# Holding side jobs to their place in the queue, splitting new weights behind the old ones' last products, and regrouping the differences of w2

## The chip, the cores and the metric

The kernel runs on one core of a Trainium2 chip. The metric is device time in microseconds (us) of one execution; three executions were timed, and one more was profiled.

## What is computed

The reference is a block-sparse attention (4 batches, 8 heads, 768 positions, head size 64), whose output, 3072 rows of 512, goes through a mixture of eight experts in which every row takes every expert:

```python
logits = x @ w_gate
P = np.exp(logits - logits.max())
for _ in range(8):
    P /= P.sum(1, keepdims=True) + 1e-09
    P /= P.sum(0, keepdims=True) + 1e-09
    P *= N / E
for e in range(E):
    h = np.maximum(x @ w1[e], 0.0)
    out += P[:, e:e + 1] * (h @ w2[e])
```

with x of 3072 x 512, w1[e] of 512 x 1024 and w2[e] of 1024 x 512, all float32.

## The kernel before

Attention runs first, to about 465 us; the rest is the mixture of experts (MoE), which the change concerns.

**Numbers.** Each float32 operand is held as a high and a low half in float16 (`h`, `w1p`, `w2p`, and x in `xp`), and a product takes three matmuls: high by high, high by low, low by high. A weight is first scaled by a power of two: eight maxima on VectorE (`mx_w`, line 187), one over them (193), a transpose on TensorE that spreads it (`all_w`, 110) and some short steps (199 to 205). Its high half comes from ScalarE (line 1011), its low half from VectorE (1015), 1024 columns each: such a pair is a split.

**Products.** Both stages use seven products in place of eight for a 2 x 2 blocked matrix product, in the order p = 0, 1, 5, 6, 3, 4, 2, so that sums and differences are needed on both sides: of weights on POOL (`queue_sum`, line 1026), of h on POOL and VectorE, and of results on VectorE.

**Stages and batches.** There are 32 batches i = (e, b), eight experts times four groups of rows. `stage1(i, qi)` makes one quarter of h: seven products of six matmuls (128 x 384, line 1135, tiles p), each read from its bank by a comb (VectorE, line 1145) or ScalarE. From the combs come the terms of h: relu on ScalarE, s and three more on POOL (lines 1207, 1033), high halves on ScalarE (1155), low halves on POOL or VectorE (1159, 1165). `stage2(i, p)` is one of seven products in three slices of twelve matmuls (128 x 256, line 1248, tiles py), and VectorE adds each slice into the result (acc, line 1269, 512 or 256 columns). The loop mixes the seven products of `stage2(i)` with the four quarters of `stage1(i + 1)`. There are four banks for p and four for py.

**Weights.** A raw weight lies in one buffer (`r`, one copy), first w1 of the next expert and, when that is split, w2 (load: line 173). The split halves overwrite the old expert's: `w1p` may be written once the last quarter of the expert's last batch has used it, `w2p` once its last stage two has. So in the last batch of an expert (b = 3) the kernel must split w1, load, measure and split w2, and go on with products.

**What sets the order.** The class `Slots` has two queues: `urgent` (sums and low halves of h) and `lazy` (weights: maxima, splits and sums). `tick`, called after each product or slice, adds what a product costs on TensorE, VectorE and ScalarE to running totals, and calls the jobs whose delay is over and whose charge (`dve=`, `act=`, `pool=`) fits under the total of TensorE plus a lead. `need` calls what a product must have. What they call is then in program order, but the framework's scheduler places each engine's instructions anew by when it simulates them to be ready, so a job may come to stand ahead of instructions that were called before it. `keep_in_program_order` holds the side jobs among themselves only.

Of the kernel before, what the change touches and what calls it, by code (L numbers as in the profile page):

```python
# [55 lines left out]
def tile_sparse_attention_moe(  # L56
# [951 lines left out]
    def queue_split(dst, src, key, delay=1):  # L1008
# [31 lines left out]
    def split_w1(e):  # L1040
# [5 lines left out]
        one(0, a[0, 0])  # L1046
        queue_sum(a[0, 0], a[1, 0], a[0, 0], ("w1", e, 5))
        one(1, a[0, 1])
        queue_sum(a[0, 1], a[0, 1], a[0, 0], ("w1", e, 2))
        one(5, a[0, 0])  # L1050
        one(6, s3)
        one(3, a[1, 1])
        one(4, a[1, 0])
        one(2, a[0, 1])

    def split_w2(e, r):
# [10 lines left out]
        one(0, m[0, 0])  # L1067
        queue_sum(m[0, 0], m[0, 1], m[0, 0], ("w2", e, 4))
        one(1, m[1, 0])
        queue_sum(t2, m[1, 1], m[0, 0], ("w2", e, 5))  # L1070
        queue_sum(m[0, 1], m[0, 1], m[1, 1], ("w2", e, 6))
        queue_sum(m[1, 0], m[1, 0], t2, ("w2", e, 3))
# [317 lines left out]
```

## Time and profile before

| | |
|---|---|
| median of 3 runs | 2357.71 us (2354.69 to 2358.62) |
| profiled execution | 2357.4 us, of which its span 2355.6 us |
| mean granted TensorE clock | 0.986 of full speed |
| TensorE / VectorE / ScalarE / POOL busy | 2200.1 / 2014.4 / 1256.0 / 1287.1 us |

The profile is of one execution. Its span is counted from the first to the last instruction, 1.8 us shorter than the execution's own time. Line numbers are those of the kernel before; engines are PE (TensorE matmul), PEld (its weight load), DVE (VectorE), ACT (ScalarE), POOL (GpSimd) and SP (the queue that issues loads). A wait is put down to the instruction whose end released it. Neighbouring instructions of one engine overlap by some 0.08 us, so that the step from start to start is a little shorter than a duration.

### The profile page before, as it was taken

Reading aid. Unit: us, or ns where it says so; the run is one execution under the profiler, and the core shown is the slowest. Engines: PE = TensorE matmul, PEld = TensorE weight load, DVE = VectorE, ACT = ScalarE, POOL = GpSimd, SP = SyncE. Lnnn points to the kernel's source line nnn. Section 1 sums busy time; section 2 is a strip of 40 time slices with the busy share of each in tenths; the row PEclk is TensorE's granted clock in tenths of the full one; section 3 lists DMA queues with packets and bytes.
Section 4 is the critical chain, followed back from the end, with each engine's and each line's share of the span. In section 5 each row is a group of like instructions: output and inputs, shape, how many; then the busy total and the mean of one; then the engine's idle time right before and its main releaser. Section 6 shows DMA issues by size and latency. Waiting matters only on the chain.

```text
span 2355.6 us, 47334 instructions
## 1 busy us (share of the span) xinstructions
PE 2200.1 (93%) x18892; PEld 1608.6 (68%) x18892; DVE 2014.4 (86%) x3570; ACT 1256.0 (53%) x2173; POOL 1287.1 (55%) x1235
## 2 busy tenths in 40 slices
PE   5999998879999999999989999999899999998999
PEld 3766666647666677677667776776677667766777
DVE  8999999888789878987898789878987898789876
ACT  4888878655465445444444445444544454445442
POOL 2012334496367645765576557655865486548543
PEclk9999999999999999999999999999999999999999
DMA  6667765422121212121212121212211221121221
GB/s 152 135 123 151 186 131 121 135 97 75 48 82 50 83 48 83 48 83 48 83 48 83 48 84 52 80 48 83 64 68 48 84 80 52 48 84 48 75 75 54
DMA packets 191888, 192.34 MB, mean 82 GB/s; under 512 B 131740, under 2 KB 144052, under 8 KB 191668
## 3 DMA queue, kind: packets, MB, share of 16 engines
q1 hardware_dynamic: 191104, 189.30, 28.2%
q8 instruction: 147, 2.41, 0.4%
q14 instruction: 73, 0.60, 0.1%
q10 hardware_dynamic: 564, 0.03, 0.0%
HBM read 140.54 MB, written 17.30 MB: 67 GB/s over the span
## 4 chain that ended last, share of the span: by engine, by line
PE 57%; DVE 21%; POOL 9%; issue 6%; DMA 4%; ACT 3%; SPq 0%; DVEq 0%; POOLq 0%; ACTq 0%
PE py L1248 25%; PE p L1135 23%; POOL r L1026 3%; DVE top L673 3%; DMA r<-in_moe_w_dram 3%; DVE h L1165 2%; PE u L731 2%; POOL h L1165 2%; DVE u L1145 2%; DVE acc L1269 2%; DVE mx_w L187 2%; PE t L697 1%; PE m L664 1%; PE t L700 1%; PE m L667 1%
## 5 line engine op out<-in xcount | busy, mean ns | idle before, releaser
L1248 PE MATMUL py<-w2p,h 128*128 128x256 f16 x8064 | 971.1, 275 | 52.7 <-ACT h L1155 23.7
L1248 PEld LDWEIGHTS <-h 128*128 128x128 f16 x8064 | 790.1, 99 | 209.9 <-ACT h L1155 28.8
L1269 DVE SCALAR_TENSOR_TENSOR acc<-py,spare,acc 128x256 f32<-128x256 f32 (+1 forms) x840 | 459.2, 581 | 49.5 <-PE py L1248 46.9
L1165 POOL TENSOR_TENSOR h<-u,h 128x384 f16<-128x384 f32 x128 | 127.0, 992 | 601.3 <-ACT h L1155 601.3
L1135 PEld LDWEIGHTS <-attic 128*128 128x128 f16 x3072 | 301.8, 98 | 195.9 <-issue 22.5
L1135 PE MATMUL p<-attic 128*128 128x384 f16 x2304 | 413.2, 328 | 16.4 <-DVE r L1145 14.4
L1135 PE MATMUL p<-arena 128*128 128x384 f16 x2304 | 407.6, 327 | 19.4 <-DVE a L1145 11.2
L1135 PEld LDWEIGHTS <-arena 128*128 128x128 f16 x2304 | 225.9, 98 | 153.5 <-issue 24.8
L1155 ACT ACTIVATE h<-c 128x384 f16<-128x384 f32 x256 | 133.6, 522 | 330.7 <-DVE c L1145 256.7
L705 ACT ACTIVATE pe<-t,shift,qk 128x768 int32<-128x768 f32 x192 | 189.7, 989 | 78.6 <-PE t L700 73.0
L1145 DVE SCALAR_TENSOR_TENSOR a<-p,a 128x384 f32<-128x384 f32 x384 | 211.1, 550 | 18.9 <-PE p L1135 14.3
L673 DVE TENSOR_REDUCE top<-m 128x1 f32<-128x768 f32 x192 | 181.8, 949 | 16.7 <-PE m L667 16.4
L1155 ACT ACTIVATE h<-r 128x384 f16<-128x384 f32 x256 | 132.5, 521 | 66.5 <-POOL r L1033 63.0
L1207 POOL TENSOR_TENSOR s<-a,u 128x384 f32<-128x384 f32 x128 | 129.6, 1013 | 68.7 <-ACT a L1204 68.7
L1033 POOL TENSOR_TENSOR r<-s,r 128x384 f32<-128x384 f32 x128 | 155.4, 1214 | 9.6
L1033 POOL TENSOR_TENSOR c<-c,r 128x384 f32<-128x384 f32 x128 | 150.8, 1178 | 10.0
L1135 PE MATMUL p<-arena,attic 128*128 128x384 f16 x768 | 146.1, 327 | 0.0
L1026 POOL TENSOR_TENSOR r<-r 128x256 f32<-128x256 f32 (+1 forms) x106 | 135.0, 1290 | 20.0 <-DVE arena L1015 17.9
L664 PE MATMUL m<-kt,qt 128*128 128x512 f16 (+1 forms) x384 | 129.6, 338 | 14.5 <-DVE top L673 7.2
L1165 POOL TENSOR_TENSOR h<-r,h 128x384 f16<-128x384 f32 x128 | 142.8, 1115 | 0.2 <-ACT h L1155 0.2
L1145 DVE SCALAR_TENSOR_TENSOR r<-p,a 128x384 f32<-128x384 f32 x128 | 70.7, 552 | 79.0 <-PE p L1135 59.4
L697 PE MATMUL t<-qt,kt 128*128 128x512 f16 (+1 forms) x384 | 127.9, 333 | 10.8 <-DVE top L673 10.6
(206 smaller groups left out, 3683.1 us busy)
## 6 DMA issues: line engine op xcount, KB each, us to landing
arena<-xd SPq DMA_DIRECT2D x128, 384.0 KB, 3.9
attic<-xd SPq DMA_DIRECT2D x96, 384.0 KB, 3.9
r<-in_moe_w_dram SPq DMA_DIRECT2D x16, 2048.0 KB, 8.4
arena<-in_q_dram SPq DMA_DIRECT2D x16, 384.0 KB, 4.5
arena<-in_k_dram SPq DMA_DIRECT2D x16, 384.0 KB, 4.8
arena<-in_v_dram SPq DMA_DIRECT2D x4, 1536.0 KB, 8.5
xd<-xs_t SPq DMA_DIRECT2D x16, 384.0 KB, 4.6
out_dram<-acc SPq DMA_DIRECT2D x24, 256.0 KB, 2.0
```

The costliest lines, as they stand in the source:

```text
L664: nc.tensor.matmul(sc[:, lo:hi], lhsT=qt[:, 0, c], rhs=ka[:, lo:hi], start=True, stop=False)
L673: nc.vector.tensor_reduce(out=tops[n][:, c : c + 1], in_=sc[:, :S], axis=AX.X, op=ALU.max)
L697: nc.tensor.matmul(sc[:, lo:hi], lhsT=kt[:, 0, c], rhs=qa[:, lo:hi], start=True, stop=False)
L705: nc.scalar.activation(pe, sc[:, :S], AF.Exp, bias=shift, scale=qk[n // 2][3])
L1026: lambda c=c: Pinned.gpsimd.tensor_tensor(out=out[:, c], in0=x[:, c], in1=y[:, c], op=op),
L1033: nc.gpsimd.tensor_tensor(out=out, in0=x, in1=y, op=ALU.subtract)
L1135: nc.tensor.matmul(ps, lhsT=w1p[p][:, l, kc, fs], rhs=xp[p][:, r, kc], start=(kc == 0 and m == 0), stop=(kc == KH - 1 and m == 2),)
L1145: nc.vector.scalar_tensor_tensor(out=t, in0=ps, scalar=HDOWN, in1=other, op0=ALU.mult, op1=ALU.add)
L1155: nc.scalar.activation(h[:, 0], src, AF.Relu if relu else AF.Copy)
L1165: eng.tensor_tensor(out=h[:, 1], in0=src, in1=h[:, 0], op=ALU.subtract)
L1248: nc.tensor.matmul(py, lhsT=hs[i, p, kc][:, l, tsl], rhs=w2p[p][:, r, kc], start=(kc == 0 and m == 0), stop=(kc == KF // 2 - 1 and m == 2),)
L1269: nc.vector.scalar_tensor_tensor(out=dst, in0=src, scalar=c, in1=dst, op0=ALU.mult, op1=ALU.add)
```

## The change

1. `not_earlier(fn)`: when a lazy job of a weight (keys `scale`, `w1`, `w2`) is called, each instruction it makes on VectorE, ScalarE or POOL is tied to the last instruction of its engine that was called before it and is no side job. The tie is one of order on the same engine and brings no wait on a semaphore; the scheduler can place the job later, but not ahead of that instruction.
2. `split_w1` returns its jobs by product and in pairs with their differences; `stage1` calls those of p behind the product p, in the last quarter of the last batch that uses the old weight (`used`). Before, all jobs were queued at the start of the expert's last batch's loop round. The order of the new weight's parts is 0, 1, 6, 5, 3, 4, 2, and no longer 0, 1, 5, 6, 3, 4, 2.
3. Load, maxima and first jobs of w2 are queued ahead of the next batch's first quarter, not behind it.
4. `split_w2` forms its differences in another way: t1 = m01 − m00 and m01 − m11 need no scale and are queued with the maxima; the two others, m11 − t1 and m10 less that, follow the first split. Product 4's source is now t1, product 5's is in m00. There are still four differences.
5. Charges and delays: a maximum 0.65 for 0.6 (first delay 8 for 6), a high half 1.1 for 1.04, a low half 1.4 for 1.2, a difference 3.2 for 2.4, a low half of h on POOL 1.05 for 0.9, the sums of h 4.4 for 3.9.

```diff
+    def not_earlier(fn):
+        made = nc.cur_bb.bb.instructions
+        n = len(made)
+        fn()
+        for ins in list(made[n:]):
+            if ins.engine not in SIDE:
+                continue
+            for old in reversed(made[:n]):
+                if old.engine == ins.engine and old.name not in aside:
+                    tc.add_manual_dep(ins, old.name, behind, reason="not_ahead_of_its_place")
+                    break
+            aside.add(ins.name)
...
-            fn, _, _, costs, _ = queue.pop(n)
+            fn, key, _, costs, _ = queue.pop(n)
+            self.charge(costs)
...
-            self.charge(costs)
-            fn()
+            if key[0] in ("scale", "w1", "w2"):
+                not_earlier(fn)
+            else:
+                fn()
...
-        t2 = raw.tile([P, h, DH], F32, tag="s3", name=f"t2_{e}")
+        t1 = raw.tile([P, h, DH], F32, tag="s3", name=f"t1_{e}")
...
+        def sums():
+            queue_sum(t1, m[0, 1], m[0, 0], ("scale", 2, e))
+            queue_sum(m[0, 1], m[0, 1], m[1, 1], ("scale", 2, e))
+
+        def first():
+            one(0, m[0, 0])
+            queue_sum(m[0, 0], m[1, 1], t1, ("w2", e, 5))
+            one(1, m[1, 0])
+            queue_sum(m[1, 0], m[1, 0], m[0, 0], ("w2", e, 3))
+
         return [
-            lambda: one(5, t2),
-            lambda: (one(6, m[0, 1]), one(3, m[1, 0])),
-            lambda: (one(4, m[0, 0]), one(2, m[1, 1])),
+            sums,
+            first,
+            lambda: (one(6, m[0, 1]), one(5, m[0, 0])),
+            lambda: (one(4, t1), one(3, m[1, 0]), one(2, m[1, 1])),
         ]
...
-    def stage1(i, qi):
+    def stage1(i, qi, used=None):
...
+            if used and p in used:
+                used[p]()
...
         def quarter(qi):
             if more:
-                stage1(i + 1, qi)
+                swap = qi == FH // P - 1 and b == B - 2 and nxt
+                stage1(i + 1, qi, split_w1(e + 1) if swap else None)
...
-        if last:
-            split_w1(e + 1)
         stage2(i, 0)
         stage2(i, 1)
-        quarter(0)
         if last:
             for p in range(NP):
                 slots.need(("w1", e + 1, p))
             load_w(2, e + 1)
-            if not PRE:
-                scale_w(2, e + 1)
+            parts = split_w2(e + 1, wr[2])
+            scale_w(2, e + 1)
+            parts[0]()
             queue_weight(e + 1)
-            parts = split_w2(e + 1, wr[2])
+        quarter(0)
```

The instructions are the same on every engine, in another order. Three places of it follow; a row is line, operation, output and inputs, shape.

VectorE in the last quarter of batch 15, the last that uses expert 3's w1. L1015 splits (arena and attic hold w1's parts), L1145 combs, L1269 adds the slices of the next stage two. Before:

```order
L1015 SCALAR_TENSOR_TENSOR attic<-s_4_17454,sw_4_17452,attic 128x1024
L1145 SCALAR_TENSOR_TENSOR u_15_3_18714<-p_15_3_18715,a_15_3_18685 128x384
L1165 TENSOR_TENSOR h_8094<-r_15_3_18694,h_8094 128x384
L1015 SCALAR_TENSOR_TENSOR attic<-r_4_17448,sw_4_17452,attic 128x1024
L1145 SCALAR_TENSOR_TENSOR c_15_3_18723<-p_15_3_18724,u_15_3_18714 128x384
L1015 SCALAR_TENSOR_TENSOR arena<-r_4_17448,sw_4_17452,arena 128x1024
L1015 SCALAR_TENSOR_TENSOR attic<-r_4_17448,sw_4_17452,attic 128x1024
L1145 SCALAR_TENSOR_TENSOR u_15_3_18714<-p_15_3_18734,u_15_3_18714 128x384
L1145 SCALAR_TENSOR_TENSOR a_15_3_18685<-p_15_3_18734,a_15_3_18685 128x384
L1015 SCALAR_TENSOR_TENSOR attic<-r_4_17448,sw_4_17452,attic 128x1024
L1269 SCALAR_TENSOR_TENSOR acc_10006<-py_0_0_18768,spare_16608,acc_10006 128x512 x2
L1269 SCALAR_TENSOR_TENSOR acc_10006<-py_0_1_18785,spare_16608,acc_10006 128x512 x2
```

and now (L1035 is the split, L1179 the comb, L1303 acc, L1199 and L1193 low halves of h):

```order
L1035 SCALAR_TENSOR_TENSOR arena<-r_4_17448,sw_4_17452,arena 128x1024
L1179 SCALAR_TENSOR_TENSOR a_15_3_18685<-p_15_3_18712,a_15_3_18685 128x384
L1199 TENSOR_TENSOR h_8094<-r_15_3_18698,h_8094 128x384
L1179 SCALAR_TENSOR_TENSOR u_15_3_18721<-p_15_3_18722,a_15_3_18685 128x384
L1035 SCALAR_TENSOR_TENSOR arena<-r_4_17448,sw_4_17452,arena 128x1024
L1179 SCALAR_TENSOR_TENSOR c_15_3_18734<-p_15_3_18735,u_15_3_18721 128x384
L1035 SCALAR_TENSOR_TENSOR attic<-s_4_17454,sw_4_17452,attic 128x1024
L1179 SCALAR_TENSOR_TENSOR u_15_3_18721<-p_15_3_18744,u_15_3_18721 128x384
L1179 SCALAR_TENSOR_TENSOR a_15_3_18685<-p_15_3_18744,a_15_3_18685 128x384
L1193 SCALAR_TENSOR_TENSOR h_8101<-c_15_3_18734,h_8101 128x384
L1303 SCALAR_TENSOR_TENSOR acc_10006<-py_0_0_18779,spare_16716,acc_10006 128x512 x2
L1179 SCALAR_TENSOR_TENSOR a_15_3_18685<-p_15_3_18756,a_15_3_18685 128x384
```

The splits that stood in one run ahead of the first acc rows stand one by one between combs, and acc begins while four parts are still to be split.

POOL at the same change of expert, later, around the term s of batch 16's fourth quarter (L1207). L1026 are the differences of w2 (r is the raw weight, t the extra tile, 256 columns each). Before:

```order
L1026 TENSOR_TENSOR t_4_18963<-r_4_18957 128x256
L1165 TENSOR_TENSOR h_8089<-c_16_2_19232,h_8089 128x384
L1026 TENSOR_TENSOR r_4_18957<-r_4_18957 128x256
L1026 TENSOR_TENSOR t_4_18963<-r_4_18957 128x256
L1026 TENSOR_TENSOR r_4_18957<-r_4_18957 128x256
L1026 TENSOR_TENSOR r_4_18957<-r_4_18957,t_4_18963 128x256 x3
L1165 TENSOR_TENSOR h_8112<-u_16_3_19424,h_8112 128x384
L1026 TENSOR_TENSOR r_4_18957<-r_4_18957,t_4_18963 128x256
L1207 TENSOR_TENSOR s_16_3_19468<-a_16_3_19390,u_16_3_19424 128x384
L1033 TENSOR_TENSOR a_16_3_19390<-a_16_3_19390,r_16_3_19400 128x384
L1033 TENSOR_TENSOR r_16_3_19400<-s_16_3_19468,r_16_3_19400 128x384
L1033 TENSOR_TENSOR c_16_3_19434<-c_16_3_19434,r_16_3_19400 128x384
```

and now (L1046 the differences, L1241 s, L1053 the other sums of h, L1199 low halves):

```order
L1053 TENSOR_TENSOR c_16_2_19234<-c_16_2_19234,r_16_2_19203 128x384
L1199 TENSOR_TENSOR h_8100<-r_16_2_19203,h_8100 128x384
L1199 TENSOR_TENSOR h_8089<-c_16_2_19234,h_8089 128x384
L1046 TENSOR_TENSOR t_4_18883<-r_4_18881 128x256
L1046 TENSOR_TENSOR r_4_18881<-r_4_18881 128x256 x4
L1046 TENSOR_TENSOR r_4_18881<-r_4_18881,t_4_18883 128x256 x4
L1199 TENSOR_TENSOR h_8112<-u_16_3_19419,h_8112 128x384
L1241 TENSOR_TENSOR s_16_3_19465<-a_16_3_19379,u_16_3_19419 128x384
L1053 TENSOR_TENSOR a_16_3_19379<-a_16_3_19379,r_16_3_19389 128x384
L1053 TENSOR_TENSOR r_16_3_19389<-s_16_3_19465,r_16_3_19389 128x384
L1053 TENSOR_TENSOR c_16_3_19430<-c_16_3_19430,r_16_3_19389 128x384
```

Fewer differences stand ahead of s, but nine in one block without a low half between them; four more come behind s and what follows it.

POOL in the first quarters of MoE, where expert 0's w2 is split as well. Before:

```order
L1026 TENSOR_TENSOR t_0_8197<-r_0_7728 128x256
L1026 TENSOR_TENSOR r_0_7728<-r_0_7728 128x256
L1165 TENSOR_TENSOR h_8095<-c_0_0_8159,h_8095 128x384
L1026 TENSOR_TENSOR t_0_8197<-r_0_7728 128x256
L1026 TENSOR_TENSOR r_0_7728<-r_0_7728 128x256
L1026 TENSOR_TENSOR t_0_8197<-r_0_7728 128x256
L1026 TENSOR_TENSOR r_0_7728<-r_0_7728 128x256
L1165 TENSOR_TENSOR h_8098<-u_0_1_8235,h_8098 128x384
L1026 TENSOR_TENSOR r_0_7728<-r_0_7728,t_0_8197 128x256
L1207 TENSOR_TENSOR s_0_1_8281<-a_0_1_8198,u_0_1_8235 128x384
L1026 TENSOR_TENSOR r_0_7728<-r_0_7728,t_0_8197 128x256 x3
L1033 TENSOR_TENSOR a_0_1_8198<-a_0_1_8198,r_0_1_8209 128x384
```

and now:

```order
L1199 TENSOR_TENSOR h_8094<-r_0_0_8130,h_8094 128x384
L1199 TENSOR_TENSOR h_8095<-c_0_0_8159,h_8095 128x384
L1046 TENSOR_TENSOR t_0_8197<-r_0_7728 128x256
L1199 TENSOR_TENSOR h_8098<-u_0_1_8233,h_8098 128x384
L1241 TENSOR_TENSOR s_0_1_8277<-a_0_1_8198,u_0_1_8233 128x384
L1053 TENSOR_TENSOR a_0_1_8198<-a_0_1_8198,r_0_1_8208 128x384
L1053 TENSOR_TENSOR r_0_1_8208<-s_0_1_8277,r_0_1_8208 128x384
L1053 TENSOR_TENSOR c_0_1_8244<-c_0_1_8244,r_0_1_8208 128x384
L1199 TENSOR_TENSOR h_8101<-r_0_1_8208,h_8101 128x384
L1199 TENSOR_TENSOR h_8102<-c_0_1_8244,h_8102 128x384
L1199 TENSOR_TENSOR h_8105<-u_0_2_8317,h_8105 128x384
L1241 TENSOR_TENSOR s_0_2_8360<-a_0_2_8283,u_0_2_8317 128x384
```

The differences went out of the quarters 0 to 2 of batch 0; all but one stand behind them.

## Rows read from the trace of the kernel before

**Rows 1.** The page: busy time and share of the engines; load of a weight.

```profile
PE 2200.1 (93%) x18892; PEld 1608.6 (68%) x18892; DVE 2014.4 (86%) x3570; ACT 1256.0 (53%) x2173; POOL 1287.1 (55%) x1235
...
r<-in_moe_w_dram SPq DMA_DIRECT2D x16, 2048.0 KB, 8.4
```

**Rows 2.** The chain that ended last: start us, us, engine, tile, line, instructions.

```profile
1149.09 3.91 PE p L1135 x24
...
1376.00 7.31 PE py L1248 x67
1383.32 3.91 PE p L1135 x24
...
2084.37 3.91 PE p L1135 x24
```

**Rows 3.** Stretches: us, PE, PEld, DVE, ACT, POOL, PEclk, DMA, GB/s.

```profile
1401.40:1404.40 3.00, 3.00 (x15) 2.13 (x16) 3.00 (x6) 0.52 (x1) 0.00 (x0) 0.50 0.92 270
...
1480.00:1616.90 136.90, 136.90 (x1057) 103.28 (x1056) 108.72 (x204) 62.58 (x126) 80.98 (x80) 1.00 0.12 41
478.10:517.20 39.10, 26.11 (x149) 15.18 (x149) 31.30 (x39) 21.49 (x40) 36.71 (x33) 0.91 0.36 129
501.70:507.50 5.80, 5.77 (x21) 2.90 (x21) 5.24 (x7) 4.46 (x9) 5.72 (x6) 0.55 0.33 76
```

**Rows 4.** Timeline of PE, switch: start us, us, instruction [idle before <-releaser].

```profile
1398.87 1.14 PE L1135 MATMUL p<-arena 128*128 128x384 f16 x6 [1.65 <-DVE a L1145]
1401.39 5.47 PE L1248 MATMUL py<-w2p,h 128*128 128x256 f16 x34 [1.38 <-DVE acc L1269]
...
1471.28 1.05 PE L1248 MATMUL py<-w2p,h 128*128 128x256 f16 x8 [3.22 <-ACT h L1155]
```

**Rows 5.** Timeline of DVE, from the last quarter of batch 15 on.

```profile
1385.35 1.28 DVE L1015 SCALAR_TENSOR_TENSOR arena<-r,sw,arena 128x1024 f16<-128x1024 f32 x1 [1.51 <-ACT arena L1011]
...
1387.02 2.05 DVE L1015 SCALAR_TENSOR_TENSOR arena<-r,sw,arena 128x1024 f16<-128x1024 f32 x1
1388.99 0.55 DVE L1145 SCALAR_TENSOR_TENSOR a<-p,a 128x384 f32<-128x384 f32 x1
...
1396.62 1.27 DVE L1015 SCALAR_TENSOR_TENSOR attic<-r,sw,attic 128x1024 f16<-128x1024 f32 x1
1397.81 0.55 DVE L1145 SCALAR_TENSOR_TENSOR u<-p,u 128x384 f32<-128x384 f32 x1
1398.28 0.54 DVE L1145 SCALAR_TENSOR_TENSOR a<-p,a 128x384 f32<-128x384 f32 x1
...
1399.94 2.71 DVE L1269 SCALAR_TENSOR_TENSOR acc<-py,spare,acc 128x512 f32<-128x512 f32 x4
...
1442.97 0.92 DVE L1285 TENSOR_TENSOR spare<-pw,pcb 128x24 f32<-128x24 f32 x1
```

**Rows 6.** DVE groups by form, whole span: busy us, mean ns.

```profile
L1165 DVE TENSOR_TENSOR h<-s,h 128x384 f16<-128x384 f32 x128 | 106.8, 834 | 27.3 <-ACT h L1155 27.1
...
L187 DVE TENSOR_REDUCE mx_w<-r 128x1 f32<-128x512 f32 x128 | 79.1, 673 | 16.1 <-DMA r<-in_moe_w_dram 16.1
...
L1015 DVE SCALAR_TENSOR_TENSOR w2p<-r,sw,w2p 128x1024 f16<-128x1024 f32 x48 | 78.3, 1634 | 12.0 <-ACT w2p L1011 12.0
```

**Rows 7.** Timeline of POOL, the w2 differences of the switch.

```profile
1446.84 5.37 POOL L1026 TENSOR_TENSOR r<-r 128x256 f32<-128x256 f32 x4
...
1465.00 1.71 POOL L1026 TENSOR_TENSOR r<-r,t 128x256 f32<-128x256 f32 x1
1466.67 0.99 POOL L1207 TENSOR_TENSOR s<-a,u 128x384 f32<-128x384 f32 x1
```

**Rows 8.** Timeline of PE in the first quarters of MoE.

```profile
487.22 0.50 PE L1248 MATMUL py<-w2p,h 128*128 128x256 f16 x3 [2.07 <-DVE h L1165]
...
491.94 2.11 PE L1135 MATMUL p<-attic 128*128 128x384 f16 x12 [1.85 <-DVE r L1145]
...
501.73 2.08 PE L1135 MATMUL p<-arena 128*128 128x384 f16 x6 [5.72 <-DVE c L1145]
```

More of the change, by code (lines that the diff above doesn't have):

```diff
@@ L996, in need @@
                     self.run(queue, 0)
+    ET = mybir.EngineType
+    SIDE = (ET.DVE, ET.Activation, ET.Pool)
     slots = Slots()
@@ L1002, in scale_w @@
         for k, part in enumerate(parts):
-            slots.add(part, key, 6 if k == 0 else 1, True, dve=0.6)
+            slots.add(part, key, 8 if k == 0 else 1, True, dve=0.65)
         slots.add(whole, key, 1, True, dve=0.1)
@@ L1018, in queue_split @@
             ),
-            key, delay + 1, True, dve=1.2,
+            key, 1, True, dve=1.4,
         )
@@ L1028, in queue_sum @@
                 ),
-                key, 1, True, pool=2.4 / n,
+                key, 1, True, pool=3.2 / n,
             )
@@ L1044, in one, with second, third @@
             queue_split(w1p[p], src, ("w1", e, p))
[L1046 to L1054, printed above, removed]
+        def first():
+            one(0, a[0, 0])
+            queue_sum(a[0, 0], a[1, 0], a[0, 0], ("w1", e, 5))
+        def second():
+            one(1, a[0, 1])
+            queue_sum(a[0, 1], a[0, 1], a[0, 0], ("w1", e, 2))
+        def third():
+            one(6, s3)
+            one(5, a[0, 0])
+        return {
+            0: first, 1: second, 6: third,
+            3: lambda: one(3, a[1, 1]), 4: lambda: one(4, a[1, 0]), 2: lambda: one(2, a[0, 1]),
+        }
     def split_w2(e, r):
@@ L1061, in split_w2, with first @@
         }
-        t2 = raw.tile([P, h, DH], F32, tag="s3", name=f"t2_{e}")
+        t1 = raw.tile([P, h, DH], F32, tag="s3", name=f"t1_{e}")
         def one(p, src):
             queue_split(w2p[p], src, ("w2", e, p))
[L1067 to L1072, printed above, removed]
+        def sums():
+            queue_sum(t1, m[0, 1], m[0, 0], ("scale", 2, e))
+            queue_sum(m[0, 1], m[0, 1], m[1, 1], ("scale", 2, e))
+        def first():
+            one(0, m[0, 0])
+            queue_sum(m[0, 0], m[1, 1], t1, ("w2", e, 5))
+            one(1, m[1, 0])
+            queue_sum(m[1, 0], m[1, 0], m[0, 0], ("w2", e, 3))
         return [
-            lambda: one(5, t2),
-            lambda: (one(6, m[0, 1]), one(3, m[1, 0])),
-            lambda: (one(4, m[0, 0]), one(2, m[1, 1])),
+            sums,
+            first,
+            lambda: (one(6, m[0, 1]), one(5, m[0, 0])),
+            lambda: (one(4, t1), one(3, m[1, 0]), one(2, m[1, 1])),
         ]
@@ L1171, in emit @@
             if p in lop:
-                slots.add(low, key, delay, pool=0.9)
+                slots.add(low, key, delay, pool=1.05)
             else:
@@ L1215, in stage1 @@
         s1 = fresh("s1")
-        slots.add(add, (("sum", i), i, qi), 1, act=0.41, pool=3.9)
+        slots.add(add, (("sum", i), i, qi), 1, act=0.41, pool=4.4)
         emit(4, s1, delay=SD[0])
@@ L1350, in tile_sparse_attention_moe @@
         if last:
-            parts[1]()
+            parts[2]()
         quarter(2)
@@ L1355, in tile_sparse_attention_moe @@
         if last:
-            parts[2]()
+            parts[3]()
         quarter(3)
```

5 lines of the change are left out of this document (3 added, 2 removed).

## The prediction, made before the changed kernel ran

> **What bounds the kernel now.** I read the page first, then the chain of waits, then the stretches, then the timelines. The page gives TensorE 93% of the span [rows 1]; attention ends near 465 us and the rest is MoE. In the chain nearly every MoE row is TensorE, and two rows give its full speed: 24 products' matmuls of stage one in 3.91 us, 0.1627 us each, and 67 of stage two in 7.31 us, 0.1091 us each [rows 2]. One expert is 672 and 1008 of them: 109.3 + 110.0 = 219.3 us. The chain's row that opens the last quarter of an expert's last stage one comes at 1149.09 and, four experts later, at 2084.37 [rows 2]: 935.28 / 4 = 233.8 us an expert. So **14.5 us are lost at each change of expert**, and there are seven. They lie in one place: from 1480.00 to 1616.90 TensorE is busy for 136.90 of 136.90 us, with VectorE at 108.72 of them, 79% [rows 3]. The loss is in the 97 us before, where the next expert's two weights are measured and split beside the products.
>
> The timeline of TensorE shows it [rows 4]: waits of 1.65 and 1.38 us for VectorE at 1398.87 and 1401.39, then 3.00 us at a granted clock of 0.50, 1.2 GHz [rows 3]; 3.22 us for ScalarE's h at 1471.28 [rows 4], and smaller ones between. The first pair has its cause in VectorE's queue: split halves of the new w1 stand there one behind the other, and the sums of stage two (acc) come only at 1399.94 [rows 5]. The 3.22 us come over ScalarE from POOL: its 16 sums of w2 start at 1446.84, and s, from which those h are made, runs only at 1466.67, behind the last of them [rows 7].
>
> A second place is the start of MoE. The stretch 478.10 to 517.20 holds 102 matmuls of stage one and 47 of stage two, 16.6 + 5.1 = 21.7 us at full speed, in 39.10 us [rows 3]: **17.4 us lost**, 5.72 of them in one wait for VectorE, 2.07 and 1.85 in two others [rows 8], and 5.80 us at a clock of 0.55 [rows 3].
>
> **The change, part by part.** No engine gets an instruction more or less; every term is a matter of order, and the new raised charges work through the order alone.
>
> *The rule that holds side jobs, with the splits behind old products.* VectorE's splits now stand one at a time between combs (L1145 of before) and acc rows, not seven in a row. Each is taken at the step from start to start: a comb 0.47 us (1398.28 − 1397.81), an acc of 512 columns 2.71 / 4 less a little overlap, 0.66, one of 256 columns 0.40, an estimate from it; a split 1.19 us (1397.81 − 1396.62) at best and 1.97 (1388.99 − 1387.02) at worst [rows 5]; a low half of h 0.83 − 0.07 = 0.76; a maximum 0.6 [rows 6]. For the split I take 1.55, the group's mean of 1.63 less an overlap of 0.08 [rows 6]. The sum starts with the last quarter's first product, at 1383.32 in the run shown [rows 2], and VectorE's first row of it comes 2.1 us later, about where it came before (1385.35 [rows 5]).
>
> 1. The third product of batch 16, p5, whose part is now split fourth: ahead of and with that split VectorE has 7 combs (3.3), 4 splits (6.2), 4 low halves (3.0), 6 + 1 acc (4.4): 2.1 + 16.9 = 19.0 us. TensorE gets there after 56 stage-one and 72 stage-two matmuls, 9.1 + 7.9 = 17.0. It waits 2.0 us (0.6 with splits at 1.19, 3.7 at 1.97). That replaces 1.65 + 1.38 us and, as I take it, the 1.5 us that the half clock cost.
> 2. The splits of w1 now end some 8 us later, and the single raw buffer puts w2's load behind them; a load takes 8.4 us [rows 1], and eight maxima behind it wait about 1 us. Up to the transpose that TensorE does for w2's scale VectorE has 22 combs, 7 splits, 12 low halves, 12 + 9 acc, 8 maxima and that wait: 10.3 + 10.9 + 9.1 + 11.5 + 4.8 + 1.0 + 2.1 = 49.7 us; TensorE, with 24 products (six matmuls, 0.976) and 17.5 slices (twelve, 1.31), 46.3. Lost so far 3.4. On SP's queue that load keeps its place between the x loads of two batches, so it makes nothing wait that did not wait before.
> 3. Up to the comb behind w2's sixth split: 42 combs, 13 splits, 24 low halves, 22 + 24 acc, 8 maxima, ten scale steps of 2.2 (0.92 the longest [rows 5], the others at 0.14, an estimate), waits of 1.0 and 2.1: 19.7 + 20.2 + 18.2 + 24.1 + 4.8 + 2.2 + 3.1 = 92.3 us. TensorE needs the bank that this comb frees four products later, after 47 products and 392 matmuls of stage two: 45.9 + 42.8 = 88.7. Lost 3.6; I take 4.5, since each step was costed at mean prices and waits do not average out.
>
> To these 4.5 I add 1.5 us for a stretch at half clock or small waits, what the half clock cost before. About **6 of 14.5 us stay** per change: 8.5 × 7 = 59.5 us saved. With splits at their ends, 13 × 0.4 = 5 us up or down, 1 to 11 stay; 4 to 8, the forecast's own range, are half of that.
>
> *POOL's sums regrouped.* Of the 16, three go ahead of batch 16's third quarter, nine behind it and four behind s of the fourth. One took 5.37 / 4 = 1.34 us in the first block [rows 7], 1.71 at most [rows 7], and the 16 ran from 1446.84 to 1466.67 with other work between them, so under 1.2 on the mean. Nine at 0.95, an estimate between, are 8.6 us; a quarter brings POOL at most 81 / 10 = 8.1 us of other work in its 13.7 us (80.98 us in 136.90, some ten quarters [rows 3]), of which I take 7.5, since that stretch holds a few sums too. That is 2 us too much for one quarter, which its neighbours, with 6 us of POOL free in each, take up: nothing. If that cover is gone, s is late and TensorE waits (rival C).
>
> *The start.* TensorE's order is now three whole quarters, 126 matmuls or 20.5 us, ahead of any product of stage two, and POOL's sums go behind them. The waits of 5.72, 2.07 and 1.85 us and the 2.6 us that the clock of 0.55 cost go: 12.2 us. New: POOL's 7.5 us a quarter against TensorE's 42 × 0.1627 = 6.8, three times, 2 us. **10 us saved**, 3 (only the longest wait goes, half of it coming back) to 14.
>
> **Sum:** 2357.4 − 59.5 − 10 = 2287.9. The profiled execution, 2357.4, is 0.3 under the median of 2357.71; I forecast **2288 us**.
>
> **A rule against it.** A split's step was 1.19 us in one place and 1.97 in another [rows 5], with POOL idle beside the first and working beside the second. The Trainium skill's page "SBUF — State Buffer", section "Who interferes with whom", says that a VectorE instruction with two SBUF inputs and a GpSimd instruction that reads SBUF exclude each other, one waiting for the other's end; splits and low halves are of that kind. The two rows agree with it. By the rule splits spread over a longer time meet POOL more often.
>
> **Rivals.**
>
> *A: VectorE at its slow prices.* All splits at 1.97 and not 1.55 add 13 × 0.42 = 5.5 us a change: 6 + 5.5 = 11.5 stay, 3 × 7 = 21 saved, with the start 31: 2326, or 2310 if half of it comes. For: the splits spread over more of POOL's time. Against: the mean of 1.63 [rows 6] already holds splits that met POOL. The Trainium skill's rule weighed above would, if every split meets POOL, give this time.
>
> *B: nearly all is gone.* Splits at 1.25: the sum's losses vanish, 1 to 2 us stay, 13 × 7 + 14 = 105 saved: 2253 (to 2266). For: the acc rows are free early, and four banks let TensorE run ahead. Against: VectorE's own sums above reach TensorE's.
>
> *C: slower.* Nine sums in one block ahead of s of the fourth quarter at 1.70 us are 15.3 us, with 7.5 of POOL's other work 22.8 in a quarter of 13.7 us: 9 us late, of which one is covered; TensorE waits 8 us more and loses 2.6 us to half clock, as at the start: 6 + 10.6 = 16.6 against 14.5 of now. 2.1 × 7 = 15, less 10: 2362. It decides from sums of about 1.6 us on. Against: of the 16, the mean is under 1.2.
>
> *D: it does nothing that counts.* The order on paper changes, but the same weight work meets the same 97 us with VectorE nearly full, and each wait returns elsewhere: 2357.
>
> **Chances.** Forecast 0.60 (2270 to 2302), A 0.20, B 0.10, C 0.06, D 0.04. The range takes forecast and A and leaves out B, C and D: 2266 to 2327. A measurement can tell about 0.2%, 4.7 us, from no change: faster 0.90, same 0.04, slower 0.06.
>
> **What would show it.** Right: chain rows that open an expert's last quarter stand about 225 us apart and not 233.8; in VectorE's timeline no two splits of w1 stand together ahead of the acc rows; TensorE's first wait after them is under 3 us; the 5.72 us wait at the start is gone. A: splits with a mean near 2 us. C: a wait of over 8 us for h, with POOL in a block of nine sums before it. Wrong altogether: periods of 233 us or more, with waits of new names.

## The result and the profile after

The changed kernel takes **2333.93 us** (median of 4 runs, 2332.60 to 2336.78), the one before 2356.38 in the runs beside it: ratio 0.9906, 95% interval 0.9889 to 0.9923. It is 22.4 us faster. 2288 had been forecast, 69 us faster, with a range from 2266 to 2327: the sign was right, the size three times too large, and the time lies 7 us above the range.

The page after (busy time and share of the engines):

```profile
PE 2192.4 (94%) x18892; PEld 1607.8 (69%) x18892; DVE 1999.7 (86%) x3570; ACT 1255.6 (54%) x2173; POOL 1289.9 (55%) x1235
```

TensorE is busy 7.7 us less than in [rows 1], VectorE 14.7 us less, with the same instructions.

Where the 24.8 us between the two profiled spans (2355.6 and 2330.8) came from can be read off three points in time. The first product of MoE started at 462.2 us before and at 455.4 us now; the order up to there is the same on every engine, and in the twelve other profiled kernels of this study, whose attention part is the same too (but for shorter maxima in one), it lay between 454.7 and 461.8. So these 6.8 us are the spread of the attention part from run to run, not a gain of the change. From there to the last quarter of expert 0's last stage one it took 218.16 us before and 216.45 now: 1.7 us for the start. From there to the end it took 1675.2 us before and 1659.0 now: 16.2 us for the seven changes of expert. Before (start us, us, line, instruction; the starts count, since a row is cut where the view ended):

```profile
462.22 0.99 PE L1135 MATMUL p<-arena 128*128 128x384 f16 x4
...
680.38 0.81 PE L1135 MATMUL p<-arena 128*128 128x384 f16 x4
```

and now:

```profile
455.39 4.08 PE L1167 MATMUL p<-arena 128*128 128x384 f16 x18
...
671.84 0.33 PE L1167 MATMUL p<-arena 128*128 128x384 f16 x1
```

So the pair of profiles shows a gain of some 18 us behind attention; the medians differ by 22.4, with an interval of 18 to 26 us. TensorE's timeline has the last quarter of batch 11 and, four experts later, that of batch 27:

```profile
1135.41 3.09 PE L1167 MATMUL p<-arena 128*128 128x384 f16 x18
...
2060.82 3.09 PE L1167 MATMUL p<-arena 128*128 128x384 f16 x18
```

(2060.82 − 1135.41) / 4 = 231.35 us an expert, against 233.82 in [rows 2]: 2.5 us saved at each change. 225 had been forecast. At full speed an expert is 219.3, so 12.0 us are still lost per change, not 6.

TensorE at the change from expert 3 to 4, the one of [rows 4] (the first row is the start of the last quarter; idle time and its releaser stand in brackets):

```profile
1366.09 3.09 PE L1167 MATMUL p<-arena 128*128 128x384 f16 x18
...
1387.31 0.82 PE L1167 MATMUL p<-arena 128*128 128x384 f16 x4 [1.75 <-DVE arena L1035]
...
1402.57 1.14 PE L1167 MATMUL p<-attic 128*128 128x384 f16 x6 [0.74 <-DVE r L1179]
...
1404.80 1.14 PE L1167 MATMUL p<-attic 128*128 128x384 f16 x6 [0.87 <-DVE a L1179]
...
1418.46 0.32 PE L110 MATMUL all_w<-ident,ma_w 128*128 128x128 f32 x1 [1.86 <-DVE ma_w L193]
...
1449.87 1.36 PE L1282 MATMUL py<-w2p,h 128*128 128x256 f16 x11 [1.62 <-DVE w2p L1035]
...
1465.15 2.11 PE L1167 MATMUL p<-attic 128*128 128x384 f16 x12 [1.82 <-DVE r L1179]
```

The pair of waits of [rows 4] for a and acc, 1.65 and 1.38 us, is gone, and the 3.22 us for ScalarE's h too. In their place stand six other waits of 0.7 to 1.9 us: for the split of w1's part p5 at 1387.31, for combs at 1402.57 and 1404.80 and, at 1418.46, for the maximum of w2 that the transpose takes, for w2's split at 1449.87 and for a comb (r) behind a split at 1465.15. They sum to 8.7 us.

VectorE in the same stretch:

```profile
1368.83 1.28 DVE L1035 SCALAR_TENSOR_TENSOR arena<-r,sw,arena 128x1024 f16<-128x1024 f32 x1
...
1372.27 1.82 DVE L1035 SCALAR_TENSOR_TENSOR arena<-r,sw,arena 128x1024 f16<-128x1024 f32 x1
...
1385.32 1.93 DVE L1035 SCALAR_TENSOR_TENSOR arena<-r,sw,arena 128x1024 f16<-128x1024 f32 x1
...
1401.37 0.69 DVE L187 TENSOR_REDUCE mx_w<-r 128x1 f32<-128x512 f32 x1 [1.74 <-DMA r<-in_moe_w_dram]
...
1462.70 1.93 DVE L1035 SCALAR_TENSOR_TENSOR w2p<-r,sw,w2p 128x1024 f16<-128x1024 f32 x1
1464.56 0.54 DVE L1179 SCALAR_TENSOR_TENSOR r<-p,a 128x384 f32<-128x384 f32 x1
```

The first four splits of w1 stand apart now, as the order showed, and the first acc row stands between them, at 1378.07; of the later ones two stand together, at 1388.43. The row at 1401.37 is the first maximum of w2; VectorE waited 1.74 us for the load, and the comb of the next quarter stood behind it. At 1462.70 w2's sixth split takes 1.93 us, and r, for which TensorE waits, comes behind it.

### The profile page after: what moved, and what is told of

The parts are those of the page before. It is cut to its first block, busy times and chain, and to the rows that moved or that the text cites. A ratio compares the mean times of both kernels' runs of the same rounds, so it can differ in the third digit from the quotient of the medians.

```text
span 2330.8 us, 47300 instructions
## 1 busy us (share of the span) xinstructions
PE 2192.4 (94%) x18892; PEld 1607.8 (69%) x18892; DVE 1999.7 (86%) x3570; ACT 1255.6 (54%) x2173; POOL 1289.9 (55%) x1235
## 4 chain that ended last, share of the span: by engine, by line
PE 48%; DVE 8%; POOL 5%; issue 3%; ACT 2%; DMA 2%; DVEq 0%; POOLq 0%; SPq 0%
PE p L1167 24%; PE py L1282 24%; DVE acc L1303 2%; POOL r L1046 2%; DMA r<-in_moe_w_dram 2%; DVE h L1199 1%; POOL h L1199 1%; DVE a L1179 1%; DVE mx_w L187 1%; ACT h L1189 1%; ACT attic L1031 1%; POOL s L1241 1%; DVE u L1179 1%; DVE attic L1035 1%; DVE w2p L1035 1%
## 5 line engine op out<-in xcount | busy, mean ns | idle before, releaser
L1282 PE MATMUL py<-w2p,h 128*128 128x256 f16 x8064 | 952.3, 273 | 19.6 <-DVE w2p L1035 7.8
L1282 PEld LDWEIGHTS <-h 128*128 128x128 f16 x8064 | 790.8, 98 | 159.7 <-issue 19.1
L1303 DVE SCALAR_TENSOR_TENSOR acc<-py,spare,acc 128x256 f32<-128x256 f32 (+1 forms) x840 | 455.1, 579 | 36.4 <-PE py L1282 35.5
L1199 POOL TENSOR_TENSOR h<-u,h 128x384 f16<-128x384 f32 x128 | 126.7, 990 | 589.8 <-ACT h L1189 589.8
L1167 PE MATMUL p<-attic 128*128 128x384 f16 x2304 | 418.5, 331 | 24.6 <-DVE r L1179 19.4
L1167 PE MATMUL p<-arena 128*128 128x384 f16 x2304 | 409.5, 327 | 16.3 <-DVE arena L1035 11.5
L1179 DVE SCALAR_TENSOR_TENSOR a<-p,a 128x384 f32<-128x384 f32 x384 | 210.8, 549 | 19.8 <-PE p L1167 15.0
L673 DVE TENSOR_REDUCE top<-m 128x1 f32<-128x768 f32 x192 | 181.6, 948 | 12.6 <-PE m L667 12.3
L1241 POOL TENSOR_TENSOR s<-a,u 128x384 f32<-128x384 f32 x128 | 130.9, 1022 | 49.1 <-ACT a L1238 48.9
L1053 POOL TENSOR_TENSOR r<-s,r 128x384 f32<-128x384 f32 x128 | 149.4, 1167 | 10.0
L1053 POOL TENSOR_TENSOR c<-c,r 128x384 f32<-128x384 f32 x128 | 149.3, 1166 | 10.0
L1046 POOL TENSOR_TENSOR r<-r 128x256 f32<-128x256 f32 (+1 forms) x106 | 135.6, 1304 | 26.6 <-DVE arena L1035 26.6
L1199 POOL TENSOR_TENSOR h<-c,h 128x384 f16<-128x384 f32 x128 | 143.3, 1120 | 3.5 <-ACT h L1189 3.5
L1179 DVE SCALAR_TENSOR_TENSOR r<-p,a 128x384 f32<-128x384 f32 x128 | 70.5, 551 | 83.4 <-PE p L1167 65.9
L1189 ACT ACTIVATE h<-s 128x384 f16<-128x384 f32 x128 | 66.9, 522 | 136.5 <-POOL s L1241 136.3
```

The costliest lines, as they stand in the source:

```text
L673: nc.vector.tensor_reduce(out=tops[n][:, c : c + 1], in_=sc[:, :S], axis=AX.X, op=ALU.max)
L1046: lambda c=c: Pinned.gpsimd.tensor_tensor(out=out[:, c], in0=x[:, c], in1=y[:, c], op=op),
L1053: nc.gpsimd.tensor_tensor(out=out, in0=x, in1=y, op=ALU.subtract)
L1167: nc.tensor.matmul(ps, lhsT=w1p[p][:, l, kc, fs], rhs=xp[p][:, r, kc], start=(kc == 0 and m == 0), stop=(kc == KH - 1 and m == 2),)
L1179: nc.vector.scalar_tensor_tensor(out=t, in0=ps, scalar=HDOWN, in1=other, op0=ALU.mult, op1=ALU.add)
L1189: nc.scalar.activation(h[:, 0], src, AF.Relu if relu else AF.Copy)
```

## Experiments

Each kernel was timed in three rounds beside the kernel before, whose medians in the three sets were 2357.1, 2357.0 and 2358.7 us. The changed kernel's own time stands above (2333.9).

### The rule alone

The kernel before with `not_earlier`, and nothing else of the change:

```diff
-            fn()
+            if key[0] in ("scale", "w1", "w2"):
+                not_earlier(fn)
+            else:
+                fn()
```

> The kernel before with the rule that holds side jobs, and nothing else of the change. Theory (the gain at a change of expert comes from splits that stand both early and apart): without the early queueing the held splits stand late, products wait for w1's parts, and the time is 2350 to 2375 us. Rival (the rule is the gain, the rest does little): 2330 to 2340 us, about that of the changed kernel (2334).

2405.69 us, ratio 1.0211 (1.0193 to 1.0230): 2.1% slower, beyond the theory's own range. TensorE's waits from 1393 to 1500 us, the change from expert 3 to 4 (us in total, times, longest):

```profile
PE p L1155 <- DVE u L1165: 4.4, 2, 4.0
PE p L1155 <- ACT attic L1031: 2.8, 1, 2.8
```

The rule keeps the jobs where they are called, and in that kernel they are called late. Products wait for w1's high halves (attic) and for combs (u): the 4.0 us come at 1457.54, for a comb that stands behind six maxima of w2 (from 1452.84 on).

### The change without the rule

```diff
-            if key[0] in ("scale", "w1", "w2"):
-                not_earlier(fn)
-            else:
-                fn()
+            fn()
```

> The changed kernel without the rule that holds side jobs; early queueing, regrouping and charges stay. Theory: the splits stand in one run ahead of the first acc rows again, as before, and the time is 2345 to 2362 us. Rival (the early queueing and the regrouping carry the gain): 2330 to 2338 us.

2361.62 us, ratio 1.0017 (1.0007 to 1.0027): as before, hardly slower. VectorE's timeline has the last splits of w1 ahead of the first acc again (L1032 the split, L1300 acc; to be read beside [rows 5]):

```profile
1395.69 1.27 DVE L1032 SCALAR_TENSOR_TENSOR arena<-r,sw,arena 128x1024 f16<-128x1024 f32 x1
1396.88 1.27 DVE L1032 SCALAR_TENSOR_TENSOR attic<-r,sw,attic 128x1024 f16<-128x1024 f32 x1
...
1399.01 1.27 DVE L1032 SCALAR_TENSOR_TENSOR attic<-r,sw,attic 128x1024 f16<-128x1024 f32 x1
1400.20 2.05 DVE L1300 SCALAR_TENSOR_TENSOR acc<-py,spare,acc 128x512 f32<-128x512 f32 x3
```

and TensorE waits 5.0 us for a high half of h in that change:

```profile
PE py L1279 <- ACT h L1186: 5.0, 1, 5.0
```

So the gain needs the rule. That the rule needs the early queueing is seen in the kernel above, which lacks the other edits too, and more closely in the next.

### Rule and regrouping, but w1's splits queued as late as before

```diff
-                stage1(i + 1, qi, split_w1(e + 1) if swap else None)
+                stage1(i + 1, qi)
...
+        if last:
+            jobs = split_w1(e + 1)
+            for p in (0, 1, 6, 3, 4, 2):
+                jobs[p]()
```

> The changed kernel with all splits of w1 queued at the start of the last batch's turn, as before, and not behind the old products; rule, regrouping and charges stay. Theory (rule and early queueing need one another): as the rule alone, 2385 to 2410 us. Rival (the regrouping and w2's earlier queueing repair it): 2330 to 2350 us.

2364.58 us, ratio 1.0027 (1.0011 to 1.0042). Neither range holds it: w2's earlier queueing, the regrouping and the charges together repair most of what the rule alone cost (2405.7; which of them does it was not tried), but the time stays 31 us over the changed kernel's. The largest wait from 1370 to 1500 us is one:

```profile
PE all_w L110 <- DVE ma_w L193: 6.3, 1, 6.3
```

Most of what was late gathers at the maximum of w2, where TensorE waits 6.3 us; six other groups of waits there sum to 4.1.

### The charges

The changed kernel with all charges and delays of before (item 5 of the change leaves one delay out: the low half of a weight is queued with a delay of 1 now and of `delay + 1` before):

```diff
-            slots.add(part, key, 8 if k == 0 else 1, True, dve=0.65)
+            slots.add(part, key, 6 if k == 0 else 1, True, dve=0.6)
...
-            key, delay, True, act=1.1,
+            key, delay, True, act=1.04,
...
-            key, 1, True, dve=1.4,
+            key, delay + 1, True, dve=1.2,
...
-                key, 1, True, pool=3.2 / n,
+                key, 1, True, pool=2.4 / n,
...
-                slots.add(low, key, delay, pool=1.05)
+                slots.add(low, key, delay, pool=0.9)
...
-        slots.add(add, (("sum", i), i, qi), 1, act=0.41, pool=4.4)
+        slots.add(add, (("sum", i), i, qi), 1, act=0.41, pool=3.9)
```

> The changed kernel with the charges and delays of before. Theory (four fresh waits of about 2 us at a change, because VectorE has no reserve in that stretch): about the same, 2328 to 2340 us. Rival (the raised charges hold maxima and w2's splits so long that TensorE waits for them): the waits for the maximum (2.0 to 2.2 us) and for w2's splits (1.1 to 2.3 us) go, 3 us or more in each of seven changes, 2310 to 2320 us.

2313.43 us, ratio 0.9812 (0.9792 to 0.9833): 20.5 us faster than with the raised ones. The theory fell and the rival's time came, but not by its way: after 640 us the wait for the maximum stayed, 12.3 us in seven against 12.5 in the changed kernel, and that for w2's splits grew, 11.5 against 7.8.

```profile
PE all_w L110 <- DVE ma_w L193: 12.3, 7, 1.9
```

Three more kernels took the charges apart.

The first three lines of that diff alone (maxima and splits):

> The changed kernel with the charges and delays of before for maxima and splits alone (0.6, 1.04, 1.2, delays 6 and +1); POOL's charges stay raised. Theory (the raised charges of the weight jobs make w2's splits late for TensorE): most of the 20 us that all old charges gave, 2313 to 2322 us. Rival (POOL's charges do it): 2330 to 2338 us.

2308.87 us, ratio 0.9803 (0.9788 to 0.9818): all of it, 25 us, 4 us below the theory's range. The last three alone (POOL):

> The changed kernel with POOL's charges of before alone (2.4, 0.9, 3.9); those of maxima and splits stay raised. Theory (weight jobs' charges): 2328 to 2338 us. Rival (POOL's charges): 2313 to 2322 us.

2330.04 us, ratio 0.9892 (0.9875 to 0.9909): 4 us, which is about what such runs differ by. The second and third line alone (splits, while maxima keep 0.65 and 8):

> The changed kernel with the charges and delay of before for splits alone (1.04, 1.2, +1); maxima keep 0.65 and 8. Theory (the splits' charge makes w1's fifth part and w2's parts late): most of the 25 us of the weight charges, 2308 to 2316 us. Rival (the maxima's): 2326 to 2336 us.

2318.22 us, ratio 0.9831 (0.9804 to 0.9858): 16 of the 25 us, somewhat outside both ranges. So it is above all the splits' charge and delay; the rest is put down to the maxima, which were not tried alone. TensorE's waits after 640 us in the kernel with the weight charges of before:

```profile
PE all_w L110 <- DVE ma_w L193: 13.2, 7, 2.1
PE py L1282 <- DVE w2p L1035: 10.3, 8, 1.5
PE py L1282 <- POOL h L1199: 7.8, 13, 0.9
```

and in the changed kernel:

```profile
PE p L1167 <- DVE r L1179: 18.0, 12, 2.5
PE all_w L110 <- DVE ma_w L193: 12.5, 8, 2.1
PE p L1167 <- DVE arena L1035: 11.5, 7, 1.8
PE py L1282 <- DVE w2p L1035: 7.8, 12, 1.6
```

The waits for w1's split (arena, seven of 1.6 us on the mean) are gone, and those for r but for 0.6 us; in their place stand 7.8 us for POOL's low halves. That for the maximum is about the same, and that for w2's splits, the theory's reason, is not shorter. All of TensorE's waits after 640 us sum to 41.5 us here and to 60.3 in the changed kernel. The rest of the 25 us is the clock: up to the last quarter of expert 7 the trace of the changed kernel has 27.3 us at a granted clock of 0.50, 13.7 us of lost work at most, and this one 6.8 us. Why the raised charges make w1's part and the comb r late, and not w2's, stays open.

### The differences of w2 grouped as before

```diff
-        t1 = raw.tile([P, h, DH], F32, tag="s3", name=f"t1_{e}")
+        t2 = raw.tile([P, h, DH], F32, tag="s3", name=f"t2_{e}")
...
+            queue_sum(m[0, 0], m[0, 1], m[0, 0], ("w2", e, 4))
             one(1, m[1, 0])
+            queue_sum(t2, m[1, 1], m[0, 0], ("w2", e, 5))
+            queue_sum(m[0, 1], m[0, 1], m[1, 1], ("w2", e, 6))
+            queue_sum(m[1, 0], m[1, 0], t2, ("w2", e, 3))
```

> The changed kernel with the four differences of w2 grouped as before (all behind the first splits). Theory: 2330 to 2340 us, no difference to be told. Rival (POOL's block of nine differences makes w2's splits late, and TensorE's wait for them of 1.1 to 2.3 us comes from it): these waits go, and the time is 2320 to 2326 us.

2323.92 us, ratio 0.9861 (0.9844 to 0.9877): 10 us faster than with the new grouping; the rival was right on the time. Of its reason half holds. The waits for w2's splits went, from 7.8 to 1.2 us, but 9.2 us came for ScalarE's reads of p's banks (a):

```profile
PE p L1165 <- ACT a L1212: 9.2, 7, 1.5
...
PE py L1280 <- DVE w2p L1035: 1.2, 2, 0.7
```

All waits after 640 us sum to 58.0 us, hardly less than 60.3; what is gone are the 27.3 us at half clock, of which there are none here before the last quarter of expert 7. So these 10 us came for the most part over the clock. With the charges of before too,

> Rule and early queueing of the change, charges and differences of before. Theory (both are losses of their own that add, 20 and 10 us): 2300 to 2308 us. Rival (both delay the same jobs, and either one undoes the delay): 2311 to 2320 us.

2326.96 us, ratio 0.9878 (0.9863 to 0.9893): not even as good as either alone. Neither expectation holds it. What the two give doesn't add: the charges of before are worth 20.5 us beside the new grouping and nothing beside the old one (2323.92 without them). That both move the same jobs is the likely reason; it was not traced. This kernel is the rule and the early queueing by themselves: 30 us faster than the kernel before (2357.0). The fastest kernels that compute everything are the change's own grouping with the weight charges of before and, no different by these runs, the last one below (2309.45).

### Less work for VectorE

Each maximum over 64 of its 512 columns, which leaves most of a weight out in finding its scale:

```diff
-                out=m[:, k : k + 1], in_=flat[:, k * w : (k + 1) * w], axis=AX.X,
+                out=m[:, k : k + 1], in_=flat[:, k * w : k * w + 64], axis=AX.X,
```

> The changed kernel with each of the eight maxima of a weight taken over 64 of its 512 columns (it leaves out the rest of the weight in finding the scale). Theory (VectorE has too much to do up to TensorE's transpose for the scale, so that a lighter VectorE is earlier there): some 8 x 0.5 us of work less per weight, TensorE's wait of 2.0 to 2.2 us before the transpose goes, 2315 to 2322 us. Rival (the maxima's place in the order or w2's later load sets it): the wait stays over 1.5 us and the time is 2328 to 2336 us.

2294.21 us, ratio 0.9737 (0.9718 to 0.9756): 40 us faster than the changed kernel, more than twice what the theory asked for. Its page and its waits after 640 us:

```profile
PE 2173.8 (95%) x18892; PEld 1603.4 (70%) x18892; DVE 1943.8 (85%) x3570; ACT 1257.2 (55%) x2173; POOL 1288.9 (56%) x1235
```

```profile
PE p L1167 <- DVE r L1179: 13.0, 12, 1.5
PE p L1167 <- DVE arena L1035: 11.5, 7, 1.8
...
PE all_w L110 <- DVE ma_w L193: 2.4, 6, 1.6
```

VectorE has 1999.7 − 1943.8 = 56 us less to do, and the time fell by 40. The wait before the transpose all but went (12.5 to 2.4 us) and r's fell; that for w1's split, which stands ahead of the maxima, is the same 11.5. Only half of the 56 us lies where it counts: of a change's sixteen maxima the eight of w2 stand in the stretch, 8 × (0.674 − 0.209) = 3.7 us less, while those of w1 come later (1504.88 to 1520.60 in the changed kernel), where TensorE waits for nothing. A change gained 40 / 7 = 5.7 us: TensorE's waits fell from 60.3 to 35.2 us in seven, 3.6 a change, and none of the 27.3 us at half clock were left, worth up to 2.0 a change. So VectorE's work is what TensorE waits for in this stretch.

### A later transpose

```diff
-        slots.add(spread, key, 1, True, gap=2)
+        slots.add(spread, key, 1, True, gap=6)
```

> The changed kernel with the transpose for a weight's scale held back (gap 6 for 2), which puts it 2.3 us of TensorE's work later in TensorE's order. Theory (each wait is a loss of its own, since TensorE starts afresh behind it): the waits of 2.0 to 2.2 us go in all seven changes and nothing takes their place, 2316 to 2322 us. Rival (one lateness that is only passed on: what is not waited for here is waited for at the next place): 2329 to 2336 us.

2319.06 us, ratio 0.9834 (0.9810 to 0.9858): 15 us faster, the theory's time. Its waits after 640 us show that the way was another:

```profile
PE py L1282 <- ACT w2p L1031: 20.5, 7, 3.1
PE p L1167 <- DVE r L1179: 13.7, 13, 1.5
PE p L1167 <- DVE arena L1035: 11.4, 7, 1.8
```

The 12.5 us before the transpose are gone, but a wait of 2.9 us for w2's high half has come in each change (20.5 us in seven), where splits of w2 had cost 7.8 on VectorE before. The waits of these two groups and of r and arena sum to 49.8 us in the changed kernel (18.0 + 12.5 + 11.5 + 7.8) and to 45.6 here. So most of the lateness was passed on, as the rival had it, and the rest of the 15 us came over the clock: up to the last quarter of expert 7 the trace has 10.2 us at half clock and not 27.3, which is up to 8.5 us of work. The same on top of the weight charges:

> The charges of before for maxima and splits, POOL's raised, and the transpose held back (gap 14), which puts it 5.9 us of TensorE's work later. Theory (waits are losses of their own): 7 x 2.0 us less than with those charges alone (2309), 2293 to 2299 us. Rival (w2's splits follow the scale and come later by as much): 2305 to 2320 us.

2309.45 us, ratio 0.9791 (0.9767 to 0.9816): nothing beyond the 2308.87 that these charges gave. There the rival's time came, and the wait before the transpose (13.2 us) is gone, but what took its place is only for a small part w2's splits (11.8 us, 10.3 without the delay). Most of it is ScalarE's reads of p's banks, 2.8 us without the delay:

```profile
PE p L1167 <- ACT a L1214: 15.6, 8, 2.4
```

## Why the prediction failed

**What held.** Both places of the loss were right, and the sign. *The third product of batch 16:* the sum gave a wait of 2.0 us for the split of p5; 1.75 was measured at 1387.31. That is in part luck, since both sides of the sum are 2 us short: up to there TensorE's trace has 62 and 83 matmuls, 19.1 us, and not 56 and 72, 17.0; and VectorE ended that split at 1387.25, 21.2 us behind the quarter's start, and not 19.0. *VectorE's work up to the comb behind w2's sixth split:* the sum had 92.3 us from the last quarter's start, of which 2.1 + 1.0 were waits and 89.2 work. Measured from 1368.23, just ahead of its first row, to 1463.20, half a microsecond into w2's sixth split (a stretch: us, PE, PEld, DVE, ACT, POOL, PEclk, DMA, GB/s):

```profile
1368.23:1463.20 94.97, 87.82 (x663) 64.48 (x662) 89.57 (x143) 48.61 (x86) 65.47 (x61) 1.00 0.24 81
```

VectorE was busy for 89.57 of 94.97 us; up to the comb at 1464.56 the split's remainder of 1.4 us belongs to it too. That is 90.9 us of work, within 2% of the sum. On the mean the prices were right, for the splits too (us busy, mean ns, idle before):

```profile
L1035 DVE SCALAR_TENSOR_TENSOR w2p<-r,sw,w2p 128x1024 f16<-128x1024 f32 x5 | 8.6, 1742 | 0.0
...
L1199 DVE TENSOR_TENSOR h<-s,h 128x384 f16<-128x384 f32 x6 | 5.5, 915 | 1.5 <-ACT h L1189 1.5
```

The thirteen splits of the change average 1.61 us, not near 2: rival A, splits at 1.97, did not come, and that the time came near its 2326 is chance. The rows agree with the page of the Trainium skill behind it ("SBUF — State Buffer", "Who interferes with whom"): the four splits with no POOL instruction beside them took 1.27 to 1.28 us, as that at 1368.83, and seven of the nine that met one 1.74 to 2.10, as that at 1385.32, which met low halves of h. In the other two meetings, 1.28 us at 1433.23 and 1.30 at 1452.53, POOL's difference took 1.7 us in place of 0.7. The mean of 1.61 is that mix. Rival B did not come either, and C's block of nine differences did, but cheaply:

```profile
1432.34 1.04 POOL L1046 TENSOR_TENSOR t<-r 128x256 f32<-128x256 f32 x1
1433.34 5.12 POOL L1046 TENSOR_TENSOR r<-r 128x256 f32<-128x256 f32 x4
1438.42 2.79 POOL L1046 TENSOR_TENSOR r<-r,t 128x256 f32<-128x256 f32 x4
```

Nine took from 1432.34 to 1441.21, 8.9 us, 0.99 each against the 0.95 of the estimate, and s came at 1442.04 without a wait of TensorE for h. Nearest to what came is D in its mechanism, each wait returning elsewhere, though not in its time: over the seven changes TensorE's waits after 640 us sum to 71.9 us before and to 60.3 now, 10.3 and 8.6 a change, under other names.

**The step that failed: "Lost 3.6; I take 4.5".** That step set VectorE's work against TensorE's, with 3.1 us in which VectorE does nothing: 2.1 ahead of its first row and 1.0 at the load. In the run it did nothing for 94.97 − 89.57 = 5.4 us behind that row: 1.74 at the load of w2, 2.5 in four waits for ScalarE's high halves of h, 0.3 for a product, the rest in steps of a tenth. That is 4.4 more than the 1.0 that I had, and where VectorE is the longer one it is lost. With 4.4 more of idle time and 1.7 more of work the sum's 92.3 us become 98.4; the comb came at 1464.56 − 1366.09 = 98.5. Against the 88.7 us of TensorE (the trace has the same 282 and 392 matmuls) that is 9.8 us lost and not 3.6, where the six waits of TensorE's timeline sum to 8.7. The 0.9 that I put on top for waits that do not average out was the right thought at a fifth of its size. That VectorE's work counts in this stretch is shown by the short maxima; that its idle steps make up the difference is this sum, and was not tried by an experiment that takes only them away. Nor is VectorE alone on the way: the chain of waits, followed back from the comb at 1464.56, passes over the load of w2 (8.72 us from 1392.63) and over POOL's four differences behind s, 1.43 us each:

```profile
1448.73 5.70 POOL r L1046 x4
```

**The clock.** I allowed 1.5 us per change for a stretch at half clock and small waits together. It is more: 12.0 us of loss in a period, less 8.6 of waits, leaves 3.4 us, of which the 27.3 us at half clock in the seven changes are up to 2.0 a change. Before there were 34.1 us, up to 2.4 a change, so the change took away 1.7 us of waits and 0.5 of half clock. In the change from expert 3 to 4 the changed kernel had none, as the 1.00 in the row above shows. The mean granted clock of the whole span, attention included, rose from 0.986 to 0.988 and not to full; the kernels faster than the changed one had 0.989 to 0.995.

**The start: 10 us forecast, 1.7 measured.** The stretch is in TensorE's timeline:

```profile
477.98 2.08 PE L1167 MATMUL p<-arena 128*128 128x384 f16 x6 [0.92 <-DVE a L1179]
...
510.88 0.49 PE L1282 MATMUL py<-w2p,h 128*128 128x256 f16 x3 [3.94 <-ACT w2p L1031]
```

The waits of [rows 8] are gone, but what came in their place is not what I had forecast. I had POOL as the new bound, with 2 us for three quarters. What came is that stage two now waits for the splits of w2. Its first product starts at 498.95, just behind its own split; the second waits 3.94 us at 510.88 for a high half that ScalarE makes at 509.66. It is the rule that holds them back: in the kernel without it ScalarE makes the first five from 473.54 on, and TensorE has no wait for them. The 2.08 us for six matmuls at 477.98 show that the half clock did not go either: from the first product to the last quarter of expert 0 the trace has 7.2 us at a granted clock of 0.50 before and 12.3 now. The step that failed is "New: POOL's 7.5 us a quarter": I looked for who else was slow, and not at when the moved job itself was needed next.

**"The new raised charges work through the order alone".** True as far as the rows go, and the order that was summed held them, so their price was in the sum. But beside the new grouping they cost 20.5 us, and the new grouping beside them 10 us: in the forecast neither had a line of its own. The rule and the early queueing by themselves gave 30 us (2326.96; the rule alone 2405.7, the change without it 2361.6), of which charges and grouping together took back 7.

## What to carry to other kernels

Where an engine that works in order is the longer one over a stretch, set its work *and* its idle time against the other engine's: price each place where it must wait for a load, a bank or a third engine; in the sum here none of it was made good later in the stretch. When a job is held back, look first at who needs its result next, and only then at whom it no longer disturbs. Edits that come together should be costed alone and in pairs: here the raised charges cost 20 us beside one grouping and nothing beside the other, where the whole gave 22.

## What was unexpected of the hardware

The half clock does not follow from a wait's length. TensorE's two transposes at the changes to expert 2 and expert 3 waited 2.08 us each, behind the same order of instructions:

```profile
956.17 0.32 PE L110 MATMUL all_w<-ident,ma_w 128*128 128x128 f32 x1 [2.08 <-DVE ma_w L193]
...
1187.05 0.32 PE L110 MATMUL all_w<-ident,ma_w 128*128 128x128 f32 x1 [2.08 <-DVE ma_w L193]
```

and the three microseconds behind them ran at 1.00 and 0.63 of full clock:

```profile
956.20:959.20 3.00, 3.00 (x19) 1.88 (x20) 3.00 (x7) 0.93 (x2) 0.63 (x1) 1.00 0.00 0
1187.10:1190.10 3.00, 3.00 (x13) 1.55 (x14) 3.00 (x7) 0.92 (x2) 0.62 (x1) 0.63 0.03 5
```

So of 14.5 us (before) or 12.0 us (now) lost in a change, a microsecond or two can come or go between changes of one and the same run; the seven periods of the changed kernel lie between 230.2 and 232.8 us.
